# First group's stacks loaded in a place of their own, the last two gelu blocks moved beside attention, the last tile stored in halves

## The chip, the cores and the metric

The kernel runs on one core of a Trainium2 chip. Its engines are TensorE (PE in the profile, with PEld for its weight loads), VectorE (DVE), ScalarE (ACT), GpSimd (POOL) and SyncE (SP), which here only issues DMAs. The metric is the device time of one execution in microseconds (us), as the median of several runs.

## The reference

`x` has 2048 rows (tokens) and 512 columns, all float32. Two branches are computed from it and mixed row by row:

```python
g = sigmoid((x * gate_w).sum(-1, keepdims=True))
a = attention(x)      # 32 heads of 16 columns, softmax(q k^T / 4) v, then @ wo
h = layernorm(x)
u = gelu(einsum("bsd,sf->bdf", h, w1) + b1)   # over the tokens: S = 2048 -> F = 1792
b = einsum("bdf,fs->bds", u, w2) + b2         # F -> S
out = g * a + (1 - g) * b
```

## The kernel before

Every float32 matrix product is made from three products of rounded parts: a value is split into `hi` (a rounded copy, `float32r`) and `lo` (what is left), and `hi*hi`, `hi*lo` and `lo*hi` are summed in PSUM. `split` (L66 and L67) makes the two parts: the copy to `hi` is a CAST in the profile, the subtraction a TENSOR_TENSOR.

The work goes through these stages, one after another on TensorE:

1. **Transposes and v** (0 to about 52 us).
2. **Projections** of keys and of the first half of the queries (`project`, L358), until 122 us. Their parts go to DRAM (`kp`, `qp`). Layernorm of the first eight row chunks is made beside it (`ln_load`, `ln_rows`): rows `x` are loaded into three buffers, normalised into `hf`, and split into `h_hi` and `h_lo`.
3. **First layer of the mixer** (L449 to L469), until 277 us. The 1792 columns of w1 are done in blocks of 512, the last of 256: `n` = 4 (in the last block 2) accumulators `ps[i]` of one PSUM bank each, for 16 chunks of 128 rows, so there are 64 chunks in all, the last 16 of them half as wide. A chunk is `3 n` matmuls of 512 columns. Chunk by chunk a weight block is loaded (`w_raw`, four buffers, L145, SP queue), cast to `w_hi` on ACT and subtracted to `w_lo` on POOL (three buffers each); `weight()` works a few chunks ahead. When a block is done, its four accumulators go through `gelu` (L421), a generator of seven steps that is woven into the next blocks: the bias add on DVE (L426), a square on ACT (L428), two operations on DVE (L430, L431), tanh on ACT (L433), one operation on DVE (L435), the cast to `u_hi` on ACT (L437) and the subtraction to `u_lo` on DVE (L439). The gelu of the last two accumulators (blocks 12 and 13 of u) comes after the last chunk (L470).
4. **Attention and the second layer together** (L899 to L1047), until about 1245 us. There are 32 groups (two heads and half of the queries each) of four phases, so 128 phases; an order written out by hand (`manual_schedule`) fixes what each engine does when. A phase has 16 score matmuls, numbered n = 0 to 15 here (L982), each from the stacked keys `ks` and queries `qs` of its group into one of seven PSUM banks. DVE copies scores 1, 3, 5 and 7 to SBUF (`pe`, L999) and ACT takes their exponentials in one go at the end of the phase (L1014, 2048 columns). ACT takes scores 0, 2, 4, 6, 8 and 9 from PSUM one by one (L1003) and the rest in pairs (L944; in the first phase of a group one pair is taken as two singles, L947). Then 64 small matmuls (L872; 40 in the very first phase) multiply the exponentials by v into `av`, and DVE adds `av` to the group's sum (L894). Beside each score runs, on the other half of TensorE's rows, one matmul of the second layer or of another dense job, into the bank `dn` (L991). `calls` and `later` hold what is done at the start and at the end of a given phase; `second_layer(0)` is spread over phases 0 to 5 and reads blocks 12 and 13 of u in phases 4 and 5, and the first `late_query` (phases 6 and 7) reads `big0` and `big1`, which `load_xt` brings at phase 1 (L784).
5. **The end** (from `ps_end` to the last `finish`): the last groups are projected with wo, and `finish` (L1106) multiplies by the gate, adds the mixer's row tile and stores 128 rows of the output.

**The stacks around the change.** A group's stack `ks` is six DMAs of 128 KB and two memsets of 16 rows (`shift_rows`, L487); `qs` is eight DMAs of 64 KB (`stack`, L498). Before, `ks0`, `ks1` and two `qs` buffers lie in a pool `stk` (L480) that is opened after the first layer, at addresses that the first layer's `h_hi` and `h_lo` hold until their last chunks. The memsets of `ks0` are on POOL (L493), after the last weight split of the layer. The DMAs are issued at the start of the attention loop (L900), all on SP's one queue, in the order in which they are called.

Of the kernel before, what the change touches and what calls it, by code (L numbers as in the profile page):

```python
# [59 lines left out]
def gated_mix(ctx: ExitStack, tc: tile.TileContext, a_x, a_wqkv, a_wo, b_w1, b_b1, b_w2, b_b2, gate_w, out):  # L60
# [294 lines left out]
    bd.tile([P, 56], F32, name="pad", bufs=1)  # L355
    with tc.tile_pool(name="ln0", bufs=3, side="right") as ln:

# [18 lines left out]
        for b in range(ND):  # L376
            wk_b, wq_b = qk_w.pop(0), qk_w.pop(0)
            kmax = bd.tile([P, NQ], F32, name="kmax")
            for at, (n, keys) in enumerate(jobs):
# [12 lines left out]
                if at in (2, 5):  # L392
                    c = 2 * b + at // 3
                    ln_load(ln, c)
                    ln_rows(ln, c)
                if at in (3, 4):
# [16 lines left out]
    def layer(ps, hi, lo, rhs, first, last):  # L413
        for i, p in enumerate(ps):
            wh, wl = hi[:, i * P : (i + 1) * P], lo[:, i * P : (i + 1) * P]
            for k, (a, b) in enumerate(((wh, rhs[0]), (wh, rhs[1]), (wl, rhs[0]))):
                nc.tensor.matmul(p, a, b, start=first and k == 0, stop=last and k == 2)  # L417

    with tc.tile_pool(name="ln1", bufs=3, side="right") as ln, tc.tile_pool(name="gl", bufs=2, side="right") as gl:

# [22 lines left out]
        for c in range(AHEAD):  # L443
            ln_load(ln, NH + c, AHEAD + 1)


        STEPS = 7
        gelus = []
        for f0, cs in order.items():  # L449
            n = min(NB, F - f0) // P  # L450
            ps = [bank() for _ in range(n)]
            in_order = f0 == 0 or f0 + NB >= F
            if not in_order:
                for step in gelus:
                    list(step)
                gelus = []
            with tc.manual_schedule(engines=beside) if in_order else ExitStack():
                for at, c in enumerate(cs):
                    hi, lo = weight()

                    if f0 == 0 and AHEAD < c <= NH:
                        ln_load(ln, NH + c - 1, AHEAD + 1)
                    if f0 == 0 and AHEAD < c <= NH + AHEAD:
                        ln_rows(ln, NH + c - AHEAD - 1)
# [17 lines left out]
    out_pool = att_ctx.enter_context(tc.tile_pool(name="ot", bufs=2, reuse_waits="tile"))  # L482
    QW = 2 * NB
    NP = H // 2
    k_bufs = [stk.tile([P, S], F32R, name=f"ks{i}", bufs=1) for i in range(2)]

    def shift_rows(engine, t):  # L487
        for i in range(2):
            engine.memset(t[i * HALF + SHIFT[0] : i * HALF + SHIFT[0] + DH].bitcast(F32), -1.0)


    with tc.issue_after(subs[-1].ins):
        shift_rows(nc.gpsimd, k_bufs[0])  # L493


    landed = []

    def stack(dst, src, which, pair, planes):  # L498
        b, r0 = divmod(pair * 2 * DH, P)
        for i in range(2):  # L500
            rows = slice(r0 + i * DH, r0 + (i + 1) * DH)
            for row, *part in planes:
                at = slice(i * HALF + row, i * HALF + row + DH)
                landed.append(nc.sync.dma_start(dst[at].bitcast(F32), src[b][part[which], rows, :]))

    def load_k(g):
        t = k_bufs[g % 2]
        stack(t, kp_d, 1, g % NP, PAIRS)
        return t

    def load_q(g):
        half, pair = divmod(g, NP)
        t = stk.tile([P, QW], F32R, name="qs")
        stack(t, qp_d[half], 0, pair, [*PAIRS, SHIFT])
        return t
# [267 lines left out]

    call(1, load_xt, 2)  # L784
    for b in range(ND):
# [265 lines left out]
    with (  # L1051
# [161 lines left out]
```

## Time and profile before

| | |
|---|---|
| time, median of 3 runs | 1280.51 us (1280.42 to 1280.55) |
| the profiled execution | 1280.37 us, its span 1278.4 us |
| PE busy | 1262.8 us (99% of the span) |
| ACT busy | 1081.4 us (85%) |
| DVE busy | 684.0 us (54%) |
| POOL busy | 201.8 us (16%) |
| DMA | 152.35 MB, mean 119 GB/s |

The profile is that of one execution, and its times count from the start of its span. A row of a timeline has the start, the duration, the engine, the line, the operation, `out<-in` by the program's names with partitions and columns, the number of instructions merged into it, and in brackets how long the engine was idle before and what ended that wait. A row of the chain has start, duration and what ran; the chain is followed back from the last instruction, at each step to what released it. SPq and ACTq rows are DMA issues, not transfers.

### The profile page before, as it was taken

Reading aid. Unit: us, or ns where it says so; the run is one execution under the profiler, and the core shown is the slowest. Engines: PE = TensorE matmul, PEld = TensorE weight load, DVE = VectorE, ACT = ScalarE, POOL = GpSimd, SP = SyncE. Lnnn points to the kernel's source line nnn. Section 1 sums busy time; section 2 is a strip of 40 time slices with the busy share of each in tenths; the row PEclk is TensorE's granted clock in tenths of the full one; section 3 lists DMA queues with packets and bytes.
Section 4 is the critical chain, followed back from the end, with each engine's and each line's share of the span. In section 5 each row is a group of like instructions: output and inputs, shape, how many; then the busy total and the mean of one; then the engine's idle time right before and its main releaser. Section 6 shows DMA issues by size and latency. Waiting matters only on the chain.

```text
span 1278.4 us, 33281 instructions
## 1 busy us (share of the span) xinstructions
PE 1262.8 (99%) x13342; PEld 835.1 (65%) x13342; DVE 684.0 (54%) x1149; ACT 1081.4 (85%) x1569; POOL 201.8 (16%) x318
## 2 busy tenths in 40 slices
PE   9999999989999999999999999999999999999998
PEld 7888888865666666666666666666666666666556
DVE  5675444174546454545555465545554455457663
ACT  4443344269999999999999999999999999999990
POOL 0220444462010111010101101111111111000000
PEclk9999999989999999999999999999999999999999
DMA  4798533255654454554343444443553443366611
GB/s 132 263 332 294 165 92 90 83 128 154 182 132 99 88 105 82 155 93 96 76 97 91 94 102 83 88 87 70 115 101 67 86 110 64 55 160 182 147 58 69
DMA packets 100559, 152.35 MB, mean 119 GB/s; under 512 B 17109, under 2 KB 56171, under 8 KB 96300
## 3 DMA queue, kind: packets, MB, share of 16 engines
q1 hardware_dynamic: 99820, 149.08, 46.5%
q8 instruction: 108, 1.77, 0.6%
q10 hardware_dynamic: 576, 1.05, 0.2%
q14 instruction: 55, 0.45, 0.1%
HBM read 105.39 MB, written 44.68 MB: 117 GB/s over the span
## 4 chain that ended last, share of the span: by engine, by line
PE 97%; ACT 1%; DMA 1%; issue 0%; DVE 0%; SPq 0%; ACTq 0%
PE av L872 30%; PE s L982 24%; PE acc L417 12%; PE t L982 12%; PE acc L74 8%; PE s L872 5%; PE dn L991 3%; PE pa L1065 2%; ACT p L944 1%; PE acc L198 1%; PE acc L267 0%; DMA qs<-qp 0%; ACT p L1003 0%; DMA ks<-kp 0%; ACT pe L1014 0%
## 5 line engine op out<-in xcount | busy, mean ns | idle before, releaser
L1003 ACT ACTIVATE p<-s 128x512 f32<-128x512 f32 x768 | 416.5, 809 | 1.6 <-PE s L982 1.6
L944 ACT ACTIVATE p<-t 128x1024 f32<-128x1024 f32 x352 | 369.3, 1290 | 0.0
L982 PE MATMUL s<-qs,ks 64*128 64x512 f32 x1344 | 345.5, 401 | 6.7 <-DMA qs<-qp 6.1
L999 DVE COPY pe<-s 128x512 f32<-128x512 f32 x512 | 318.4, 684 | 8.4 <-PE s L982 7.8
L982 PEld LDWEIGHTS s<-qs,ks 64*128 64x128 f32 x1344 | 239.3, 185 | 101.5 <-issue 51.9
L872 PE MATMUL av<-p,v 128*32 128x256 f32 x4904 | 288.1, 379 | 0.0
L1014 ACT ACTIVATE pe<-pe 128x2048 f32<-128x2048 f32 x129 | 279.8, 2172 | 0.0
L894 DVE TENSOR_TENSOR ot<-av,ot 128x512 f32<-128x512 f32 (+2 forms) x140 | 84.8, 606 | 364.1 <-PE av L872 363.8
L872 PEld LDWEIGHTS av<-p,v 128*32 128x32 f32 x4904 | 159.4, 110 | 105.3 <-ACT p L1003 0.3
L991 PE MATMUL dn<-u_hi,w_hi 64*128 64x512 f32 x448 | 183.4, 409 | 0.0
L991 PE MATMUL dn<-u_lo,w_hi 64*128 64x512 f32 x448 | 182.6, 408 | 0.0
L991 PE MATMUL dn<-u_hi,w_lo 64*128 64x512 f32 x448 | 181.8, 406 | 0.0
L982 PE MATMUL t<-qs,ks 64*128 64x512 f32 x704 | 179.3, 442 | 1.7
L67 POOL TENSOR_TENSOR w_lo<-w_raw,w_hi 128x512 fp32r<-128x512 f32 (+1 forms) x128 | 152.9, 1200 | 121.9 <-ACT w_hi L66 100.6
L982 PEld LDWEIGHTS t<-qs,ks 64*128 64x128 f32 x704 | 89.9, 184 | 86.6 <-ACT p L1003 86.6
L995 POOL MEMSET token<- 1x1 f32 x128 | 11.4, 89 | 834.8 <-PE dn L991 786.1
L872 PE MATMUL av<-pe,v 128*32 128x256 f32 x2048 | 137.3, 385 | 0.1
L66 ACT CAST w_hi<-w_raw 128x512 fp32r<-128x512 f32 (+1 forms) x67 | 38.0, 569 | 81.9 <-PE acc L417 62.6
L872 PEld LDWEIGHTS av<-pe,v 128*32 128x32 f32 x2048 | 53.5, 109 | 54.8 <-ACT p L1003 32.3
L417 PE MATMUL acc<-h_hi,w_hi 128*128 128x512 f32 x224 | 87.9, 392 | 0.0
L417 PE MATMUL acc<-h_hi,w_lo 128*128 128x512 f32 x224 | 87.8, 392 | 0.0
L417 PE MATMUL acc<-h_lo,w_hi 128*128 128x512 f32 x224 | 87.8, 392 | 0.0
(152 smaller groups left out, 1479.7 us busy)
## 6 DMA issues: line engine op xcount, KB each, us to landing
w_raw<-in_B_w_dram SPq DMA_DIRECT2D x96, 256.0 KB
ks<-kp SPq DMA_DIRECT2D x192, 128.0 KB
qs<-qp SPq DMA_DIRECT2D x256, 64.0 KB
x<-in_A_x_dram SPq DMA_DIRECT2D x32, 256.0 KB
kp<-pc SPq DMA_DIRECT2D x16, 512.0 KB
qp<-pc SPq DMA_DIRECT2D x8, 768.0 KB
qp<-row SPq DMA_DIRECT2D x24, 256.0 KB
v<-v SPq DMA_DIRECT2D x4, 1088.0 KB
```

What stands on the lines that cost most here:

```text
L66: copy(hi, src)
L67: return sub(lo, src, hi.bitcast(F32), ALU.subtract)
L74: nc.tensor.matmul(ps, a, b, start=start and n == 0, stop=stop and n == last)
L417: nc.tensor.matmul(p, a, b, start=first and k == 0, stop=last and k == 2)
L872: mm = nc.tensor.matmul(av[32 * j : 32 * (j + 1), i * QC : (i + 1) * QC], vb[b][:, v_at : v_at + 32], pt[:, h * QC : (h + 1) * QC], start= ...
L894: nc.vector.tensor_tensor(x, y, x, ALU.add)
L944: nc.scalar.activation(pt, twos[low, low + 1], AF.Exp, scale=SCALE)
L982: nc.tensor.matmul(s, kt[grp][rows_i, c * P : (c + 1) * P], qt[grp][rows_i, qb * NB : (qb + 1) * NB], start=True, stop=True,)
L991: mm = nc.tensor.matmul(ps, a[half], b[half], start=begin and not second, stop=last and bool(second))
L999: nc.vector.tensor_copy(pt, s)
L1003: nc.scalar.activation(pt, s, AF.Exp, scale=SCALE)
L1014: nc.scalar.activation(x, x, AF.Exp, scale=SCALE)
```

## The change

- `first_stacks`, a pool that is open from stage 2 on, holds `ks` (8 KB a partition) and `qs` (4 KB). Until the layernorm is done the same place holds its rows: four buffers `x` in `ks` (`ln_load`) and two `hf` in `qs` (`ln_rows`), in place of the pools `ln0` and `ln1`.
- At the start of the second block of the first layer (`f0 == NB`), `first_loads` sets the shift rows of `ks` on DVE and issues the 14 loads of group 0's stacks on SP. Group 1's `ks1` and `qs1` stay in `stk`; the two `qs` buffers alternate by hand.
- In the last block of the layer, `layer` goes through its two accumulators in reverse, so `ps[1]` is finished three matmuls before `ps[0]`.
- The gelu of blocks 12 and 13 is taken apart: the two bias adds stay at the end of the layer, on DVE, `ps[1]` first (`late_u`); `inner` (three DVE operations; the square is now one of them) is put at the end of phase 0 for both blocks, `tanh` (ACT) at the end of phase 1 for both, `outer` (three DVE operations; the cast to `u_hi` is now on DVE) at the end of phase 2 for the one and of phase 3 for the other. Their intermediate result is `late_s`, in the place of `big0`.
- `load_xt(2)`, which fills `big0` and `big1`, is called at phase 3 instead of phase 1.
- The bank `dn` is taken from the other end of PSUM.
- The last output tile is multiplied and stored in two halves of 256 columns, the first from ACT's queue, the second from SP's.

```diff
+    first_stacks = ctx.enter_context(tc.tile_pool(name="fs", bufs=1, reuse_waits="tile"))
+    ln_x = first_stacks.tile([P, S], F32, name="ks").rearrange("p (n d) -> p n d", d=D)
+    ln_h = first_stacks.tile([P, QW], F32, name="qs").rearrange("p (n d) -> p n d", d=D)
-    def ln_load(ln, c, bufs=3):
-        xs[c] = ln.tile([P, D], F32, name="x", bufs=bufs)
+    def ln_load(c):
+        xs[c] = ln_x[:, c % 4, :]
         nc.sync.dma_start(xs[c], xf[c * P : (c + 1) * P, :])
-    def ln_rows(ln, c):
-        hf = ln.tile([P, D], F32, name="hf", bufs=2)
+    def ln_rows(c):
+        hf = ln_h[:, c % 2, :]
...
     def layer(ps, hi, lo, rhs, first, last):
-        for i, p in enumerate(ps):
+        for i, p in list(enumerate(ps))[:: 1 if len(ps) == NB // P else -1]:
...
+        def first_loads():
+            k_bufs.append(first_stacks.tile([P, S], F32R, name="ks"))
+            q_bufs.append(first_stacks.tile([P, QW], F32R, name="qs"))
+            shift_rows(nc.vector, k_bufs[0])
+            return {0: load_k(0)}, {0: load_q(0)}
...
+            if f0 == NB:
+                kt, qt = first_loads()
...
-        for step in gelus:
-            list(step)
...
-    with tc.issue_after(subs[-1].ins):
-        shift_rows(nc.gpsimd, k_bufs[0])
...
+    late_u = []
+    for i, p in reversed(list(enumerate(ps))):
+        u = out_pool.tile([P, D], F32, name="row", bufs=3)
+        at = NF - len(ps) + i
+        nc.vector.tensor_scalar_add(u, p, b1[:, at : at + 1])
+        late_u.append((u, at))
+    late_s = o_pool.tile([P, ND, NB], F32, name="big0")
+    def inner(i):
+        u, s = late_u[i][0], late_s[:, i, :]
+        nc.vector.tensor_mul(s, u, u)
+        nc.vector.tensor_scalar(s, s, GELU_A, 1.0, ALU.mult, ALU.add)
+        nc.vector.tensor_mul(s, s, u)
+    def tanh(i):
+        nc.scalar.activation(late_s[:, i, :], late_s[:, i, :], AF.Tanh, scale=GELU_C)
+    def outer(i):
+        u, at = late_u[i]
+        nc.vector.scalar_tensor_tensor(u, late_s[:, i, :], 1.0, u, ALU.add, ALU.mult)
+        split(u_hi[:, at, :], u_lo[:, at, :], u, nc.vector.tensor_copy, nc.vector.tensor_tensor)
...
-    ps_dn = psum_ctx.enter_context(tc.tile_pool(name="ps_dn", bufs=1, space=PSUM, reuse_waits="tile"))
+    ps_dn = psum_ctx.enter_context(tc.tile_pool(name="ps_dn", bufs=1, space=PSUM, side="right", reuse_waits="tile"))
...
-    call(1, load_xt, 2)
+    for i in range(2):
+        on_dve(0, inner, i)
+        on_dve(1, tanh, i)
+        on_dve(2 + i, outer, i)
+    call(3, load_xt, 2)
...
-        kt, qt = {0: load_k(0)}, {0: load_q(0)}
...
-        for t, queue in ((1, nc.sync), (3, nc.scalar), (5, nc.sync), (7, nc.scalar)):
+        for t, queue in ((1, nc.sync), (3, nc.scalar), (5, nc.sync)):
             finish(t, queue)
+        row, gate, dst = row_of(7)
+        for cols, queue in ((slice(0, D // 2), nc.scalar), (slice(D // 2, D), nc.sync)):
+            nc.vector.scalar_tensor_tensor(row[:, cols], pa[7][:, cols], gate, row[:, cols], ALU.mult, ALU.add)
+            queue.dma_start(dst[:, cols], row[:, cols])
```

More of the change, by code (lines that the diff above doesn't have):

```diff
@@ L355, in gated_mix @@
     bd.tile([P, 56], F32, name="pad", bufs=1)
-    with tc.tile_pool(name="ln0", bufs=3, side="right") as ln:
+    if True:
         def project(w, n):
@@ L393, in gated_mix @@
                     c = 2 * b + at // 3
-                    ln_load(ln, c)
-                    ln_rows(ln, c)
+                    ln_load(c)
+                    ln_rows(c)
                 if at in (3, 4):
@@ L417, in layer @@
                 nc.tensor.matmul(p, a, b, start=first and k == 0, stop=last and k == 2)
-    with tc.tile_pool(name="ln1", bufs=3, side="right") as ln, tc.tile_pool(name="gl", bufs=2, side="right") as gl:
+    with tc.tile_pool(name="gl", bufs=2, side="right") as gl:
         def gelu(ps, fb):
@@ L443, in gated_mix, with shift_rows, stack, load_k @@
         for c in range(AHEAD):
-            ln_load(ln, NH + c, AHEAD + 1)
+            ln_load(NH + c)
+        def shift_rows(engine, t):
+            for i in range(2):
+                engine.memset(t[i * HALF + SHIFT[0] : i * HALF + SHIFT[0] + DH].bitcast(F32), -1.0)
+        landed = []
+        def stack(dst, src, which, pair, planes):
+            b, r0 = divmod(pair * 2 * DH, P)
+            for i in range(2):
+                rows = slice(r0 + i * DH, r0 + (i + 1) * DH)
+                for row, *part in planes:
+                    at = slice(i * HALF + row, i * HALF + row + DH)
+                    landed.append(nc.sync.dma_start(dst[at].bitcast(F32), src[b][part[which], rows, :]))
+        def load_k(g):
+            t = k_bufs[g % 2]
+            stack(t, kp_d, 1, g % NP, PAIRS)
+            return t
+        def load_q(g):
+            half, pair = divmod(g, NP)
+            t = q_bufs[g % 2]
+            stack(t, qp_d[half], 0, pair, [*PAIRS, SHIFT])
+            return t
+        k_bufs, q_bufs = [], []
+        def first_loads():
[3 more added lines that the diff above has]
+            return {0: load_k(0)}, {0: load_q(0)}
         STEPS = 7
@@ L461, in gated_mix @@
                     if f0 == 0 and AHEAD < c <= NH:
-                        ln_load(ln, NH + c - 1, AHEAD + 1)
+                        ln_load(NH + c - 1)
                     if f0 == 0 and AHEAD < c <= NH + AHEAD:
-                        ln_rows(ln, NH + c - AHEAD - 1)
+                        ln_rows(NH + c - AHEAD - 1)
                     layer(ps, hi, lo, (h_hi[c], h_lo[c]), at == 0, at == NS - 1)
@@ L482, in gated_mix @@
     out_pool = att_ctx.enter_context(tc.tile_pool(name="ot", bufs=2, reuse_waits="tile"))
[L483 to L489, printed above, removed]
-    with tc.issue_after(subs[-1].ins):
-        shift_rows(nc.gpsimd, k_bufs[0])
[L496 to L515, printed above, removed]
+    k_bufs.append(stk.tile([P, S], F32R, name="ks1", bufs=1))
+    q_bufs.append(stk.tile([P, QW], F32R, name="qs1", bufs=1))
     def second_out(t, ps):
@@ L782, in put_whole @@
         return put(steps, at, [len(steps)])
-    call(1, load_xt, 2)
+    for i in range(2):
+        on_dve(0, inner, i)
+        on_dve(1, tanh, i)
+        on_dve(2 + i, outer, i)
+    call(3, load_xt, 2)
     for b in range(ND):
```

2 lines of the change are left out of this document (added).

## The prediction

> **What bounds the kernel now.** I read the page's chain first, by engine, then the same chain in order of time where its PE pieces are broken.
>
> ```profile
> span 1278.4 us, 33281 instructions
> ...
> PE 97%; ACT 1%; DMA 1%; issue 0%; DVE 0%; SPq 0%; ACTq 0%
> ```
>
> ```profile
> 274.70 3.76 DMA ks<-kp
> ...
> 278.48 4.82 DMA qs<-qp
> 283.30 0.76 PE s L982
> ...
> 291.46 0.50 PE s L982
> ...
> 299.86 0.43 PE s L982
> ...
> 307.35 0.42 PE s L982
> ...
> 314.83 0.43 PE s L982
> ```
>
> TensorE carries 97% of the chain, and the DMA's 1% lies almost wholly in one place: 8.6 us (274.70 to 283.30) in which the stacks of group 0 arrive. The five PE rows start phases 0 to 4. Phases 2 and 3 take 7.49 and 7.48 us; phase 0 takes 8.16 and phase 1 8.40. So the transition costs an idle time and two slow phases. The waits of 270 to 300 us name what ended last, and the windows give the granted clock (the third figure from the end):
>
> ```profile
> PEld s L982 <- POOL ks L489: 6.5, 1, 6.5
> PE s L982 <- DMA qs<-qp: 6.1, 1, 6.1
> ```
>
> ```profile
> 280.50:283.30 2.80, 0.00 (x1) 0.04 (x1) 2.67 (x5) 1.57 (x3) 2.69 (x3) 0.50 0.98 152
> 283.30:287.20 3.90, 3.90 (x18) 3.90 (x20) 3.10 (x6) 2.60 (x5) 1.09 (x1) 0.50 0.55 116
> ```
>
> The queries' DMA came last and the POOL memset of the shift rows shortly before. Through the idle time the clock fell to 0.50, and the first 3.9 us of phase 0 ran at half speed. What follows is set by ACT:
>
> ```profile
> 275.70 0.62 ACT L66 CAST w_hi<-w_raw 128x512 fp32r<-128x512 f32 x1 [0.22 <-PE acc L417]
> ...
> 287.51 1.09 ACT L1003 ACTIVATE p<-s 128x512 f32<-128x512 f32 x2 [0.26 <-PE s L982]
> ...
> 293.04 3.10 ACT L1003 ACTIVATE p<-s 128x512 f32<-128x512 f32 x6
> 295.90 2.99 ACT L944 ACTIVATE p<-t 128x1024 f32<-128x1024 f32 x3
> ...
> 300.41 3.21 ACT L1003 ACTIVATE p<-s 128x512 f32<-128x512 f32 x6
> ```
>
> ACT waits for PE up to score 8 (287.51), then has no gap. It starts the exponentials of phase 1 at 293.04, 1.58 us after PE began that phase; for phase 2 the distance is 0.55 us (300.41 against 299.86). A distance larger by 1.03 us made phase 1 longer by 0.91 us: where ACT is late, PE pays nearly all of it. That is the price for any work put on ACT here.
>
> **The change part by part.** *The first score.* The last matmul of the first layer:
>
> ```profile
> 276.81 0.39 PE L417 MATMUL acc<-h_hi,w_lo 128*128 128x512 f32 x1
> ```
>
> With stacks and shift rows landed 100 us earlier, score 0 follows at the layer's spacing of 0.23 us, at 277.04. In the changed program it waits only for these DMAs, for the shift rows' memsets and for a DVE evacuation of the block before. What is late next is score 1: it reuses the bank of `ps[1]` and waits for its bias add; behind it stands all of phase 0 on PE. DVE's order there, then, with rows for the later steps:
>
> ```profile
> 275.51 1.37 DVE L439 TENSOR_TENSOR u_lo<-gu,u_hi 128x512 fp32r<-128x512 f32 x1 [0.71 <-ACT u_hi L437]
> 276.80 1.40 DVE L426 TENSOR_SCALAR gu<-acc,b 128x512 f32<-128x512 f32 x2
> 278.24 0.43 DVE L430 TENSOR_SCALAR gs<-gs 128x512 f32<-128x512 f32 x1
> 278.70 0.69 DVE L431 TENSOR_TENSOR gs<-gs,gu 128x512 f32<-128x512 f32 x1
> 279.31 1.49 DVE L430 TENSOR_SCALAR gs<-gs 128x512 f32<-128x512 f32 x1
> ...
> 300.62 2.48 DVE L999 COPY pe<-s 128x512 f32<-128x512 f32 x4
> ```
>
> The two bias adds are the pair at 276.80, 0.70 us each, in the new order: `ps[1]` is out at 277.5, `ps[0]` at 278.2. Score 1 comes at 277.55 instead of 277.27; the reversed order in `layer` keeps this at 0.3 us. Score 6, which needs the other bank, comes at 278.7 anyway.
>
> *ACT in phase 0.* Its third cast for the second layer has to wait for the last chunk and starts at about 277.1; at 0.5 us before the next can begin, it leaves ACT free as score 0 is ready, 277.6. Four gelu steps that stood here (two squares, two tanh) and two casts are gone. Score 2 is ready about 278.3 (issued 277.8, 0.39 us of matmul, 0.1 to be seen); from there ACT runs without a gap at 0.48 us each (295.90 less 293.04, over six), so score 8's exponential is at 278.3 + 3 x 0.48 = 279.75 instead of 287.51. The rest of the phase is unchanged: 293.04 - 287.51 = 5.53. Phase 1 starts on ACT at 285.3 instead of 293.04: 7.75 us gained, of which 6.26 is idle time, the rest slow clock and the gelu work that stood in between.
>
> *Tanh in phase 1.* 300.41 - 293.04 = 7.37 us as before, plus two tanh of 512 columns. The step of two ACT operations from SBUF to SBUF is bounded by the exponentials' 0.48 and by the whole duration of such a cast; a pair gives the value:
>
> ```profile
> 170.34 1.14 ACT L437 CAST u_hi<-gu 128x512 fp32r<-128x512 f32 x2
> ```
>
> 1.14 - 0.62 = 0.52 each, 1.04 for both (bounds 0.95 and 1.25). Nothing hides it, as ACT has no gap. Phase 2's exponentials begin at 285.3 + 7.37 + 1.04 = 293.7 instead of 300.41: **6.7 us gained**, and the later phases keep their pace.
>
> *DVE in phases 0 to 3.* Four copies 2.48, two `inner` of 0.46 + 0.61 + 0.61 = 1.7 (starts 278.24, 278.70, 279.31; the square priced as the multiplication), one add of half a bank, taken at 0.43 like the shortest of these rows: from 278.2 to 284.5. PE starts phase 1 at 291.46 - 7.75 = 283.7, its score 1 is ready at 284.5, so the next copy is not late. `outer` is three operations, by the rows above between 0.43 and 1.49 each, in a phase of 7.49 us in which the copies take 2.48: hidden, and due only in phase 4.
>
> *Queues.* SP: `load_xt` waits for the last `outer` in phase 3, about 305 on the new clock; behind it on SP stand group 2's queries and the projection weights, which are not needed before phases 6 to 8.
>
> ```profile
> 290.45 0.84 SPq L543 DMA_DIRECT2D big<-xt  x2
> ...
> 294.00:301.00 7.00, 7.00 (x90) 4.02 (x90) 2.17 (x5) 7.00 (x11) 0.82 (x2) 1.00 0.90 328
> 302.00:306.00 4.00, 4.00 (x58) 2.28 (x58) 1.10 (x2) 4.00 (x8) 0.09 (x1) 1.00 0.01 2
> ```
>
> Issued at 290.45, the 2 MB were in by 302, 12 us; 305 + 12 = 317, and phase 6 begins about 323: 6 us of cover. The first layer's loads move too: the rows `x` go ahead of weight blocks (into windows where PE has no idle time to lose), and group 0's 14 DMAs (1.28 MB) go ahead of weight chunk 20:
>
> ```profile
> 157.35 11.72 SPq L145 DMA_DIRECT2D w_raw<-in_B_w_dram  x5
> 172.02 0.62 ACT L66 CAST w_hi<-w_raw 128x512 fp32r<-128x512 f32 x1 [0.54 <-POOL w_lo L67]
> ```
>
> ```profile
> 160.00:168.00 8.00, 8.00 (x36) 6.45 (x35) 3.31 (x6) 3.75 (x6) 3.37 (x4) 1.00 0.33 98
> ```
>
> One load each 2.8 us; chunk 20 is the third of these five, issued at 163, cast at 172.02 and used at about 177.6 (two chunks of 2.8 us on). If the burst takes the 8.6 us that it took at 274.70 and most of it is issued by 160.3, chunk 20 is issued at 169 and in by 172: cost nothing.
>
> *The last tile.*
>
> ```profile
> 1271.08 0.33 SPq L1109 DMA_DIRECT2D out_dram<-base  x1
> ...
> 1273.08 0.75 DVE L1108 SCALAR_TENSOR_TENSOR base<-pa,g,base 128x512 f32<-128x512 f32 x1 [2.03 <-PE pa L1065]
> 1273.86 0.34 ACTq L1109 DMA_DIRECT2D out_dram<-base  x1
> ```
>
> ```profile
> 1271.70:1272.80 1.10, 1.10 (x6) 0.76 (x4) 0.00 (x0) 0.00 (x0) 0.00 (x0) 1.00 0.62 238
> 1274.20:1276.20 2.00, 0.00 (x0) 0.00 (x0) 0.00 (x0) 0.00 (x0) 0.00 (x0) 1.00 0.43 152
> ```
>
> The last 256 KB were on the move for 2.0 us, the tile before for 1.1. Half a tile saves between nothing and 1.0; I take half of the shorter, 0.55, less 0.05 for two shorter DVE operations instead of one: **0.5 us**. [...]
>
> **Sum:** 6.7 + 0.5 = 7.2 us. Against the profiled execution, 1280.37 (span 1278.4 and 1.97 around it, taken as unchanged), that is 1273.2; this execution lies 0.14 below the median of the runs shown, which the range covers.
>
> **Rivals.** *1. DVE gets late beside POOL* (gain 4.8, 1275.6). POOL's memsets for `ks1` (3.6 us) move with phase 0's end and now lie beside `inner`:
>
> ```profile
> 278.79 1.73 POOL L67 TENSOR_TENSOR w_lo<-w_raw,w_hi 128x512 fp32r<-128x512 f32 x1 [0.78 <-ACT w_hi L66]
> 280.57 3.82 POOL L489 MEMSET ks<- 16x2048 f32 x2
> ```
>
> ```profile
> 281.44 1.47 DVE L435 SCALAR_TENSOR_TENSOR gu<-gs,gu 128x512 f32<-128x512 f32 x2
> ```
>
> The same DVE operation that took 0.43 took 1.49 (279.31) beside the POOL subtraction at 278.79. Two `inner` scalings each held by a whole memset (1.9) make DVE late by up to 3.8; 1.4 of that is slack (PE's score 8 of phase 1, held by ACT until 286.3, needs the copy of score 1, due 284.9), the rest, 2.4, is paid. Against it: the two DVE operations at 281.44, beside that very memset, kept 0.7 us each, though they are not this operation. The Trainium skill's page "SBUF — State Buffer", section "Who interferes with whom", speaks for it: a scaling from SBUF to SBUF may use the port pair shared with GpSimd, and who comes second waits for the whole instruction. No run here yet has the pair side by side.
>
> *2. The gain is larger* (up to 8.3, 1272.1): the store saves 1.0 and tanh hides in a gap of ACT.
>
> *3. It does not do what it says* (within 2.5 us, about 1279): another input of phase 0 is late, for instance the second layer's weights, and PE waits at 277 after all. Against it: their second cast stands at 275.70 in the trace, before the layer's end.
>
> *4. Slower* (1284 or more): weight chunk 20, stuck behind the 14 stack loads on SP. It costs only from the point at which the load lands later than 175.5 (cast and subtraction before 177.6), and the sign turns when PE loses over 7.2 us, so when the burst takes some 20 us instead of 8.6. DMA was busy a third of the time there (0.33 in the window above), which speaks against it; the burst's 16-row DMAs, which run slower than the weights', speak for it.
>
> **How the numbers follow.** Forecast (gain 6.2 to 7.9) 0.62; rival 1 and dearer tanh together 0.22; rival 2 0.08; rival 3 0.04; rival 4 0.04. The range runs from rival 2 (with 0.4 us more) to rival 1 (with 0.7 more): 1271.7 to 1276.3. Faster by over 0.2% (2.56 us, about what a measurement of this kernel can tell from no change): all but rivals 3 and 4, 0.92; within 0.2% 0.04; slower 0.04.
>
> **What would show it.** Right: first score near 277.1 and the granted clock at 1.0 throughout; second score about 0.5 after it, released by a DVE add; phases 1 and 2 both near 8.4 us, with tanh between the last exponential of phase 1 and the first of phase 2; phase 3 starts near 300.6 instead of 307.35 and phases of 7.49 from there. Wrong: a wait of PE inside 122 to 277 us, a score of phase 1 released by a DVE copy, a table load between the exponentials, a wait for `big` in phase 6, or last packets as long as before.

## The result, and the profile after

The changed kernel takes **1282.38 us** (median of 20 executions, 1280.67 to 1283.80), the kernel before 1280.36 us (median of 20, 1279.49 to 1281.33): a ratio of 1.0015, 95% interval 1.0008 to 1.0021. The change makes the kernel 2.0 us slower; 1273.2 was forecast. The profiled execution of the changed kernel took 1280.95 us (span 1279.1) and is among the shortest of its 20; what the others have besides is found below.

Its page, the span and the chain by engine:

```profile
span 1279.1 us, 33309 instructions
...
PE 96%; issue 1%; ACT 1%; DVE 1%; POOL 0%; POOLq 0%; DVEq 0%
```

The DMA's 1% is gone from the chain, as the change intended: nothing waits for the first stacks any more. But "issue" (time for which the profile finds nothing that was waited for), DVE and POOL have come in. Three places hold the loss. The first is inside the first layer; the chain in order of time (start, duration, what):

```profile
172.34 6.99 issue
...
179.38 1.28 POOL w_lo L67
```

the timeline of POOL, which says what POOL stood waiting for in these 6.99 us:

```profile
179.37 3.77 POOL L67 TENSOR_TENSOR w_lo<-w_raw,w_hi 128x512 fp32r<-128x512 f32 x3 [7.43 <-ACT w_hi L66]
```

and the timeline of PE there and at the layer's end:

```profile
177.35 0.39 PE L423 MATMUL acc<-h_hi,w_lo 128*128 128x512 f32 x1
179.34 0.50 PE L423 MATMUL acc<-h_hi,w_hi 128*128 128x512 f32 x1 [1.61 <-ACT w_hi L66]
...
180.70 0.50 PE L423 MATMUL acc<-h_hi,w_lo 128*128 128x512 f32 x1 [0.62 <-POOL w_lo L67]
...
279.75 0.39 PE L423 MATMUL acc<-h_hi,w_lo 128*128 128x512 f32 x1
280.07 0.50 PE L1015 MATMUL s<-qs,ks 64*128 64x512 f32 x1
```

PE stands idle for 1.61 and 0.62 us, first for a cast of weights on ACT and then for a subtraction on POOL; the layer ends at 280.14 instead of 277.20. From the first to the last of its 672 matmuls it takes 157.65 us instead of 154.84, 2.8 more. Score 0 then follows at once. Its successors, in the chain of 277 to 305 us:

```profile
284.19 1.95 DVE big L541
...
288.80 0.43 DVE ot L928
...
289.27 0.50 PE s L1015
...
295.84 0.43 PE s L1015
...
303.77 0.43 PE s L1015
```

Phase 2 starts at 295.84 (299.86 before), phase 3 at 303.77 (307.35 before). Counted from the layer's end, phase 3 comes after 23.63 us instead of 30.15: the 6.5 us that the moved stacks and the moved gelu were to bring are there.

The second place is the end of the loop. Timeline of the changed kernel, then of the kernel before:

```profile
1241.47 1.35 PE L906 MATMUL av<-pe,v 128*32 128x256 f32 x16
...
1242.88 0.76 DVE L928 TENSOR_TENSOR ot<-av,ot 128x256 f32<-128x256 f32 x2 [1.73 <-PE av L906]
...
1243.79 0.93 PE L1098 MATMUL pa<-big,e 128*128 128x512 f32 x3 [0.97 <-DVE ot L928]
```

```profile
1244.75 1.33 PE L872 MATMUL av<-pe,v 128*32 128x256 f32 x16
...
1246.02 0.96 PE L1065 MATMUL pa<-big,e 128*128 128x512 f32 x3
```

Before, `pa` followed `av` without a gap; now it waits 0.97 us for DVE. The third place is behind the last matmul. The last matmul of the kernel before:

```profile
1272.18 0.86 PE L1065 MATMUL pa<-big,e 96*128 96x512 f32 x3
```

Timeline of the changed kernel, PE, DVE and the queues' issues:

```profile
1268.82 0.33 SPq L1142 DMA_DIRECT2D out_dram<-base  x1
...
1269.92 0.86 PE L1098 MATMUL pa<-big,e 96*128 96x512 f32 x3
1270.82 0.87 DVE L1162 SCALAR_TENSOR_TENSOR base<-pa,g,base 128x256 f32<-128x256 f32 x2 [2.03 <-PE pa L1098]
1271.33 0.34 ACTq L1163 DMA_DIRECT2D out_dram<-base  x1
1271.72 0.33 SPq L1163 DMA_DIRECT2D out_dram<-base  x1
```

The windows behind it (the last two columns are the DMA engines' busy share and GB/s):

```profile
1272.00:1273.70 1.70, 0.00 (x0) 0.00 (x0) 0.00 (x0) 0.00 (x0) 0.00 (x0) 1.00 0.50 164
1273.70:1275.00 1.30, 0.00 (x0) 0.00 (x0) 0.00 (x0) 0.00 (x0) 0.00 (x0) 0.82 0.02 6
```

The last packets of the output have ended by 1273.7, 2.9 us after the last matmul (1270.78), where it was 3.2 before (1276.2 after 1273.04). Yet the span ends at 1279.1, 8.3 us after that matmul, where it was 5.4. So the two profiled executions differ, place by place:

| | before | after | difference |
|---|---|---|---|
| last matmul of the first layer ends | 277.20 | 280.14 | +2.94 |
| from there to phase 3 | 30.15 | 23.63 | -6.52 |
| phase 3 to the last `av` | 938.73 | 939.05 | +0.32 |
| last `av` to the first `pa` | -0.06 | 0.97 | +1.03 |
| first `pa` to the last matmul's end | 27.02 | 26.99 | -0.03 |
| last matmul to the end of the span | 5.41 | 8.31 | +2.90 |
| sum | | | +0.64 |

Of the first row 0.13 us lies ahead of the layer; its start varies between 122.36 and 123.14 us in the 13 profiles of this case. What is gained once is given back in three places, none of them in attention's phases.

### The profile page after: what moved, and what is told of

Its sections match the earlier page's. It is cut to its first block, busy times and chain, and to the rows that moved or that the text cites. A ratio compares the mean times of both kernels' runs of the same rounds, so it can differ in the third digit from the quotient of the medians.

```text
span 1279.1 us, 33309 instructions
## 1 busy us (share of the span) xinstructions
PE 1263.5 (99%) x13342; PEld 832.5 (65%) x13342; DVE 688.6 (54%) x1156; ACT 1079.2 (84%) x1565; POOL 197.8 (15%) x316
## 4 chain that ended last, share of the span: by engine, by line
PE 96%; issue 1%; ACT 1%; DVE 1%; POOL 0%; POOLq 0%; DVEq 0%
PE av L906 30%; PE s L1015 23%; PE t L1015 12%; PE acc L423 12%; PE acc L74 8%; PE s L906 5%; PE dn L1024 3%; PE pa L1098 2%; PE acc L198 1%; PE acc L267 0%; ACT p L977 0%; ACT pe L1047 0%; PE pa L1128 0%; ACT p L1036 0%; PE acc L244 0%
## 5 line engine op out<-in xcount | busy, mean ns | idle before, releaser
L977 ACT ACTIVATE p<-t 128x1024 f32<-128x1024 f32 x352 | 367.0, 1271 | 0.0
```

Of the source, the lines that this page charges most:

```text
L977: nc.scalar.activation(pt, twos[low, low + 1], AF.Exp, scale=SCALE)
```

## The experiments

Each run is compared with executions of the kernel before on the same chip, whose medians were 1280.36 to 1280.44. "Tail" is the time from the end of the last matmul to the end of the span in the profiled execution.

| run | time, us | range | ratio to before, interval | tail |
|---|---|---|---|---|
| changed kernel | 1282.38 | 1280.67 to 1283.80 | 1.0015 (1.0008 to 1.0021) | 8.31 |
| a_whole | 1279.92 | 1277.97 to 1281.20 | 0.9989 (0.9980 to 0.9998) | 6.05 |
| b_act2 | 1279.25 | 1278.10 to 1281.14 | 0.9990 (0.9981 to 0.9999) | 6.66 |
| c_inorder | 1278.44 | 1277.96 to 1278.70 | 0.9983 (0.9974 to 0.9992) | 8.50 |
| d_bank | 1280.38 | 1279.81 to 1282.63 | 1.0002 (0.9993 to 1.0011) | 8.18 |
| e_all | 1274.31 | 1274.27 to 1274.78 | 0.9952 (0.9938 to 0.9965) | 5.72 |
| f_inner | 1275.12 | 1274.62 to 1275.28 | 0.9956 (0.9942 to 0.9970) | 5.81 |
| g_gelu | 1279.77 | 1278.21 to 1280.14 | 0.9991 (0.9982 to 1.0000) | 5.62 |
| h_spread | 1274.86 | 1274.50 to 1275.12 | 0.9955 (0.9942 to 0.9969) | 5.95 |
| j_sp | 1276.95 | 1276.67 to 1277.73 | 0.9974 (0.9964 to 0.9984) | 8.10 |
| k_act5 | 1274.54 | 1274.35 to 1274.78 | 0.9955 (0.9939 to 0.9972) | 5.87 |
| m_memset | 1274.48 | 1273.91 to 1275.15 | 0.9954 (0.9938 to 0.9971) | 5.57 |

**The stall in the first layer (c_inorder).** ACT's timeline in the changed kernel shows why the cast came late:

```profile
169.96 0.61 ACT L66 CAST w_hi<-w_raw 128x512 fp32r<-128x512 f32 x1
170.47 1.14 ACT L443 CAST u_hi<-gu 128x512 fp32r<-128x512 f32 x2
173.85 1.29 ACT L434 ACTIVATE gs<-gu 128x512 f32<-128x512 f32 x2 [2.23 <-DVE gu L432]
175.70 0.64 ACT L439 ACTIVATE gs<-gs 128x512 f32<-128x512 f32 x1 [0.56 <-DVE gs L437]
176.76 0.63 ACT L439 ACTIVATE gs<-gs 128x512 f32<-128x512 f32 x1 [0.43 <-DVE gs L437]
177.37 0.62 ACT L443 CAST u_hi<-gu 128x512 fp32r<-128x512 f32 x1
178.15 0.62 ACT L443 CAST u_hi<-gu 128x512 fp32r<-128x512 f32 x1 [0.17 <-DVE gu L441]
178.68 1.65 ACT L66 CAST w_hi<-w_raw 128x512 fp32r<-128x512 f32 x3
```

Before, casts stood at 172.02 and 176.11, between these gelu steps; the second of them in ACT's timeline of the kernel before:

```profile
176.11 0.60 ACT L66 CAST w_hi<-w_raw 128x512 fp32r<-128x512 f32 x1
```

Now the three casts come behind all of them, one after another and without a wait of their own: their data had been there (the last packets of the burst and of the three weight loads behind it ended at 172.4). In this block the order on ACT is not written out but made by the scheduler when the kernel is built, and with the burst ahead of the weights it put two casts behind six gelu operations. Why it chose this order is not shown; that the order is the cause is tested here and in h_spread below. The experiment keeps the burst and writes the order out:

```diff
-            in_order = f0 == 0 or f0 + NB >= F
+            in_order = f0 <= NB or f0 + NB >= F
```

> The changed kernel with the second block of the first layer in a written order on ACT, DVE and POOL too (one step of each gelu a chunk, as in the first and the last block); the 14 stack loads stay together where they are. In the changed kernel PE stood idle for 2.2 us at 178 to 181, and the cast of weight chunk 20 started at 178.68, though the packets of its load ended at 172.4. Theory (the order in which ACT takes its work): the cast comes right after the load, the idle time goes, the layer ends at 277.2 instead of about 280 and the time falls by 2.5 us (2.0 to 2.9). Rival (the load is late, or the weight pipeline has run dry behind the burst): an idle time of PE of 1 us or more remains between 172 and 190, released by a cast that itself waits for a DMA; the time falls by less than 1.2 us.

Measured: 1278.44 us, 3.9 below the changed kernel, where 2.0 to 2.9 were expected. The burst is in the same place (its issues at 156.14 to 167.50, in the changed kernel at 155.69 to 167.88), PE has no gap, and the layer ends at 277.78, 154.84 us after its start, as long as before the change. ACT's timeline:

```profile
172.59 0.62 ACT L66 CAST w_hi<-w_raw 128x512 fp32r<-128x512 f32 x1 [2.10 <-PE acc L423]
...
175.31 0.62 ACT L66 CAST w_hi<-w_raw 128x512 fp32r<-128x512 f32 x1 [1.57 <-POOL w_lo L67]
...
178.03 0.62 ACT L66 CAST w_hi<-w_raw 128x512 fp32r<-128x512 f32 x1 [1.57 <-POOL w_lo L67]
```

One cast each 2.7 us, waiting for PE or POOL and never for a DMA: the burst delays nothing, the order does. The theory holds. The gain is 1.1 us more than the 2.8 of the stall, and the range shrank from 3.1 to 0.7 us; the next runs show why.

**What the stall costs besides (a_whole, b_act2, d_bank).** These three keep the stall, and each of their profiled executions has a stretch of half clock behind it, which the profiled execution of the changed kernel has not. Windows of a_whole (the third figure from the end is the granted clock):

```profile
178.00:182.00 4.00, 1.77 (x7) 1.10 (x7) 1.76 (x3) 2.52 (x5) 2.28 (x2) 1.00 0.02 2
182.00:185.40 3.40, 3.40 (x10) 2.67 (x9) 0.00 (x0) 0.62 (x1) 1.65 (x3) 0.51 0.71 192
```

and the same stretch of the changed kernel:

```profile
182.00:185.40 3.40, 3.40 (x17) 2.81 (x16) 0.00 (x0) 0.62 (x1) 2.43 (x2) 1.00 0.69 208
```

10 matmuls instead of 17 in 3.4 us. The layer takes 159.25 us in a_whole and 159.06 and 159.07 in b_act2 and d_bank, against 157.65 in the changed kernel's profile. So the stall costs 2.8 us always and 1.4 to 1.6 more in the executions that the clock catches. That most of the 20 executions of the changed kernel belong to these is not shown by a profile of theirs, but their times fit: 13 took 1282.22 us or more and 7, the profiled one among them, 1281.83 or less. So do the ranges: 2.8 to 3.2 us in the four kernels with the stall, 0.4 to 1.2 in those without (g_gelu aside, which has a half clock elsewhere).

What decides whether the clock catches a stall can be read from the traces. In all 13 the granted clock changes only at whole multiples of 3.413 us from its first change (in a_whole at 4.58, 182.07 and 185.48 us). Divide PE's timeline into stretches of that length, from one possible change to the next, and add up PE's idle time in each: among the stretches at full clock, every one with 1.66 us or more was followed by half clock, and none with 1.63 us or less. In the changed kernel the stall fell into two stretches, with 1.13 and 1.10 us of idle time; in a_whole one stretch held 1.66, in b_act2 and d_bank 1.86. The first change lies between 4.04 and 7.09 us in the 13 profiles, so the same stall can fall either way. This is an inference from one execution of each kernel, with idle times taken from matmul ends that the profile models.

The Trainium skill's page "TensorE: Matmul & The Clock Gate", section "Part 1: The HAM clock gate (the "warmup" mystery)", has the clock halved after at least one idle window of about 3.4 us, in windows that run freely. The stretches of 3.413 us and the half clock in some profiles only agree; but here a window with 1.66 us of idle time, with matmuls beside it, was enough.

**The tail.** Three runs tell the queue from the halving. First the last tile whole on ACT's queue, as before:

```diff
-        for t, queue in ((1, nc.sync), (3, nc.scalar), (5, nc.sync)):
+        for t, queue in ((1, nc.sync), (3, nc.scalar), (5, nc.sync), (7, nc.scalar)):
             finish(t, queue)
-        row, gate, dst = row_of(7)
-        for cols, queue in ((slice(0, D // 2), nc.scalar), (slice(D // 2, D), nc.sync)):
...
```

> The changed kernel with its last tile multiplied and stored whole on ACT's queue again; nothing else differs. In the profile of the changed kernel 8.27 us pass from the first multiplication of the last tile (1270.82) to the end of the span (1279.09), before it were 5.36 (1273.08 to 1278.44), though the last packets of the tile land earlier. Theory: SP, which now issues the last store, comes later to the branch behind the last store and has to fetch the code behind it; then the distance falls back to 5.4 (5.1 to 5.7) and the time by 2.9 us against the changed kernel (1278 in the profiled run). Rival 1, the two narrow transfers are dear: the same here, told apart by the next run. Rival 2, the long end comes with the earlier end of PE or with the place of the code: the distance stays over 7.5 and the time within 0.5 us.

Measured: the tail is 6.05 us, 2.3 less (2.9 were expected; with a whole tile on ACT last the tails lie between 5.41, the kernel before, and 6.05), the time 1279.92, 2.5 below the changed kernel (both with the stall and its clock). Then both halves, but both from ACT:

```diff
-        ... ((slice(0, D // 2), nc.scalar), (slice(D // 2, D), nc.sync)):
+        ... ((slice(0, D // 2), nc.scalar), (slice(D // 2, D), nc.scalar)):
```

> The changed kernel with both halves of the last tile stored from ACT's queue, none from SP's. Theory (SP's late branch): SP is through its wait list early, ACT's branch comes at about 1.85 us after the first multiplication and its code 2.75 us later as in the kernel before, so the distance is 5.3 to 5.8 and the time 2.5 to 3.0 us below the changed kernel. Rival 1 (narrow rows of 1 KB are dear, whichever queue issues them): the distance stays at 7.8 to 8.3 and the time within 0.5 us of the changed kernel.

Measured: a tail of 6.66 us, between what the two theories gave, but 1.6 below halves on two queues; 1279.25 us. Why not 5.3 to 5.8 shows in ACT's issues:

```profile
1272.89 2.05 ACTq L1163 DMA_DIRECT2D out_dram<-base  x2
```

Two issues that take 0.34 us each alone span 2.05: the second took 1.62. By the trace's semaphore and branch records SP then waits last for ACT, which stands still behind its branch from 1275.53 to 1278.08. Halving is not free, then, but small. The clean test is a whole tile on SP, in the kernel with all three repairs (e_all, below):

```diff
-        for t, queue in ((1, nc.sync), (3, nc.scalar), (5, nc.sync), (7, nc.scalar)):
+        for t, queue in ((1, nc.scalar), (3, nc.sync), (5, nc.scalar), (7, nc.sync)):
```

> The run with all three repairs, but with the queues of the last four tiles exchanged: 1 and 5 on ACT's, 3 and the whole last tile 7 on SP's. No tile is halved. From the last matmul to the end of the span it was 5.7 us with all repairs and 8.2 to 8.5 in the runs whose second half went out on SP. Theory (SP as issuer of the last store comes late to the code behind the branch, where it alone has a list of sixteen waits): 8.0 to 8.9 us, the time 2.3 to 3.2 us above the run with the repairs (1274.3). Rival (halving was what cost): 5.5 to 6.0 us and the same time within 0.4.

Measured: a tail of 8.10 us, and 1276.95, 2.6 above e_all. SP's last issue and the last matmul in j_sp, then in e_all:

```profile
1265.94 0.86 PE L1099 MATMUL pa<-big,e 96*128 96x512 f32 x3
...
1267.61 0.33 SPq L1143 DMA_DIRECT2D out_dram<-base  x1
```

```profile
1264.88 0.33 SPq L1143 DMA_DIRECT2D out_dram<-base  x1
...
1265.98 0.86 PE L1099 MATMUL pa<-big,e 96*128 96x512 f32 x3
```

From SP's last issue to the end of the span it is 7.3 us in j_sp (1274.9), 7.4 in the changed kernel (1271.72 to 1279.1), 7.2 in d_bank and 7.6 in c_inorder, with halves and without. The trace's semaphore and branch records say what fills it. Behind its last store SP branches past a general version of attention that isn't run here (1272.66 in the changed kernel), stands still until 1275.41, goes through six waits of 0.1 us, stands still again from 1275.83 to 1277.59, and does ten more. All that it still has to wait for had landed before the first pause ended (the last store at 1274.1), and both pauses have instruction packets in them. In e_all the first pause, 2.7 us from 1265.89, lies beside the last matmul and the issue of the last store; the next stop, 1.7 us from 1268.84, is the wait for that store, which lands at 1270.5; and behind the eighth wait, where j_sp stands still for 1.6 us, it is 0.4. Before the change SP's last store was tile 5's, 2.0 us ahead of the end of the last matmul, so that its pauses lay beside other work; it waited for the last store until 1276.74 and last of all for ACT, which stood still behind its own branch from 1274.79 to 1277.54. SP's waits ended at 1277.6, 4.5 us after the last matmul. The halved tile put SP's last issue 0.9 us behind the last matmul, and its own pauses now end last: its waits are over at 1278.2, 7.4 us after the last matmul. That is the 2.9 us.

Whether SP can be freed still earlier, with tile 5 on ACT as well:

```diff
-        ... ((1, nc.sync), (3, nc.scalar), (5, nc.sync), (7, nc.scalar)):
+        ... ((1, nc.sync), (3, nc.scalar), (5, nc.scalar), (7, nc.scalar)):
```

> The run with all three repairs, but with tile 5 on ACT's queue too, so that SP's last store is tile 1's, 5.6 us earlier. Theory: SP has all its code long before the last store lands, so its pauses at 1268.84 and 1270.81 shrink to the wait for the store itself and the end comes 5.1 to 5.7 us after the last matmul: the same time to 0.6 us less than with the repairs. Rival (two stores one behind the other on ACT: the second issue took 1.62 us instead of 0.34 when both halves went that way): the last store leaves ACT 1.3 us later and the time is 0.7 to 1.3 us longer.

Measured: 1274.54 and a tail of 5.87, the same as e_all within its range. SP starts on its waits early (1262.66), but waits for the last store all the same, until 1270.61. The second issue on ACT took no longer this time, 2.8 us behind the first; so the 1.62 us of b_act2 goes with two issues close together (0.44 us from start to start). What held the second one there is not shown.

The Trainium skill's page "Perfetto Trace Analysis", section "DMA Optimizations", says that splitting a DMA may let the whole complete sooner where the DMA engines are mostly idle. They are nearly idle here (busy share 0.07 from 1271 to 1272 us in the changed kernel), and the last packets did end sooner, 2.9 us after the last matmul instead of 3.2. But neither split made the program end sooner: tails of 8.2 to 8.5 us on two queues and 6.7 on one, against 5.4 to 6.05 unsplit on ACT.

**The bank (d_bank).** The part of the change that the prediction gave no price:

```diff
-        pa = [ps_end.tile([P, D], F32, name=f"pa{t}") for t in range(8)]
+        pa = [ps_end.tile([P, D], F32, name=f"pa{t}") for t in (1, 2, 3, 4, 5, 6, 7, 0)]
+        pa = pa[-1:] + pa[:-1]
```

> The changed kernel with the end's accumulator pa0 put into the bank of dn (which is free) and the other seven moved up by one, as the banks stood before the change; nothing else differs. In the changed kernel the first pa matmul waited 0.97 us for DVE's ot, which reads the last av out of the same bank. Theory: the wait is gone, the first pa matmul follows av within 0.1 us and the time falls by 1.0 us (0.8 to 1.2). Rival: the chain from ot over the sums and the reciprocals sets the end whatever pa0 does, so the idle time only moves to a later matmul and the time falls by less than 0.4.

Measured, in the timeline of PE in d_bank:

```profile
1243.08 1.33 PE L906 MATMUL av<-pe,v 128*32 128x256 f32 x16
...
1244.33 0.96 PE L1099 MATMUL pa<-big,e 128*128 128x512 f32 x3
```

The wait is gone, and from the end of `av` to the end of the last matmul it is 26.95 us instead of 27.96: 1.0 us, as expected, with nothing behind it that took its place. The medians differ by 2.0, but both kernels still have the stall and the half clock that comes in some executions only.

**All three repairs (e_all).** Its edit is that of c_inorder, a_whole and d_bank together.

> The changed kernel with all three repairs: block 2 of the first layer in a written order, the last tile whole on ACT's queue, pa0 in the bank of dn. If the three losses are separate (theory), the gains add up: from 1278.4 (written order alone) less 2.3 (the end of 8.5 us becomes one of 6.05, as in the run with the whole tile) less 1.0 (bank) = 1275.1, within 0.6, and with it the 5 us of gain that the prediction sought are there. Rival: the losses cover each other (an earlier end of PE only waits longer for the code or the store); then it stays above 1276.5.

Measured: 1274.31 us, 0.9952 of the time before (0.9938 to 0.9965), with five executions within 0.5 us. That is 8.1 us below the changed kernel and 0.8 below the 1275.1 that was expected, 0.2 outside the margin; half a microsecond of it is the tail, which fell by 2.8 us from c_inorder's 8.50 and not by 2.3. The three losses are separate and add up. This version beats both kernels; it is 6.1 us below the kernel before, where the prediction sought 7.2.

**The burst itself (h_spread).** Instead of the written order, the 14 loads one by one:

```diff
-                    landed.append(nc.sync.dma_start(dst[at].bitcast(F32), src[b][part[which], rows, :]))
+                    put_off(nc.sync.dma_start, dst[at].bitcast(F32), src[b][part[which], rows, :])
...
+                    if f0 >= NB and todo and at % 2 == 0:
+                        start, operands = todo.pop(0)
+                        landed.append(start(*operands))
                     layer(ps, hi, lo, (h_hi[c], h_lo[c]), at == 0, at == NS - 1)
```

> Not the written order, but the other two repairs, and the 14 stack loads one by one, in every second chunk of the first layer's blocks 2 and 3 instead of all at once; the scheduler then puts the casts of weight chunks 20 and 21 on ACT where they were before the change. Theory (the place of the casts is the cause, which the scheduler chose from its own estimate of the burst): no idle time of PE at 178, the same time as with the written order within 0.4 us. Rival (the burst as such disturbs the weights): with the loads spread it is over 0.5 us faster than the written order, or, if a single stack load in front of a weight load is enough, an idle time remains.

Measured: 1274.86, no gap of PE in the layer, 0.55 above e_all (up to 0.4 was expected). The profiled executions differ by 0.12 ahead of the layer, by 0.23 in the tail and by 0.18 in the loop; no wait in the trace accounts for it, and it is left at that. Either way of keeping the casts in place ends the stall.

**DVE in phase 0 (f_inner, m_memset).** Rival 1 of the prediction did appear: `inner`'s first scaling took 1.94 us, and PE stood idle for 0.90 us in phase 1 behind a late DVE. First, less for DVE in phase 0:

```diff
-        on_dve(0, inner, i)
-        on_dve(1, tanh, i)
+        on_dve(i, inner, i)
+        on_dve(1 + i, tanh, i)
```

> The run with all three repairs, but with inner and tanh of the second of the two late blocks one phase later (phases 1 and 2 instead of 0 and 1), so that DVE has 2.0 us less to do in phase 0, where it held the ot addition back until 288.80 and PE stood idle for 0.90 us in phase 1. Theory (ACT is the bound there, it had no gap from 288.28 to 296): the idle time of PE shrinks and the time is the same within 0.3 us. Rival (rival 1 of the prediction, a late DVE is paid by PE): 0.6 to 0.9 us faster than the run with the three repairs.

Measured: the gap of PE shrinks from 0.90 to 0.40; from the layer's end to phase 4 it is 30.88 us against 31.04 in e_all: 0.16 less, so the idle time was worth next to nothing. The median, 1275.12, is 0.8 above e_all; by the profiled executions 0.6 of that arises ahead of the layer and 0.4 behind phase 4, which the edit doesn't touch. Then POOL's memset out of the way:

```diff
-            if p == 0:
+            if p == 2:
                 shift_rows(nc.gpsimd, k_bufs[1])
```

> The run with all three repairs, but with POOL's two memsets of ks1's shift rows after phase 2 instead of after phase 0. The first inner's scaling on DVE took 1.94 us in phase 0, beside a memset of 1.9 us; the second took 0.68. Theory (DVE's scaling is held while the memset runs): the first now takes 0.43 to 0.7, the ot addition comes about 1.3 to 1.5 us earlier and the idle time of PE in phase 1 (0.90) goes; the time stays within 0.3 us, as ACT is what bounds phase 1. Rival (the scaling is slow by itself, or by the copies before it): it still takes over 1.5 us.

Measured: 1274.48, the same as e_all. PE's idle time in phase 1 did not go but shrank to 0.40 us, in which PE waits for ACT, and phase 4 comes 30.88 us after the layer's end, as in f_inner. DVE and POOL in the changed kernel:

```profile
284.19 1.94 DVE L541 TENSOR_SCALAR big<-big 128x512 f32<-128x512 f32 x1
```

```profile
284.04 3.83 POOL L455 MEMSET ks<- 16x2048 f32 x2
```

and DVE in m_memset:

```profile
281.95 0.43 DVE L541 TENSOR_SCALAR big<-big 128x512 f32<-128x512 f32 x1
...
283.75 0.43 DVE L541 TENSOR_SCALAR big<-big 128x512 f32<-128x512 f32 x1
```

The scaling is held while the first memset runs (it ends at 285.84, the scaling at 286.13) and takes 0.43 without it. That settles the mechanism of rival 1, and its price: no more than 0.2 us, since ACT bounds phase 1 and has no gap there. The rule that the prediction cited from the Trainium skill's page "SBUF — State Buffer" agrees: who comes second waits for the whole instruction.

**The moved gelu (g_gelu).** e_all with the gelu of the last two blocks at the end of the layer again; only the stacks are early:

```diff
+        for step in reversed(gelus):
+            list(step)
     h_ctx.close()
...
-    late_u = []
...
-        on_dve(0, inner, i)
-        on_dve(1, tanh, i)
-        on_dve(2 + i, outer, i)
-    call(3, load_xt, 2)
+    call(1, load_xt, 2)
```

> The run with all three repairs, but with the gelu of the last two blocks whole at the end of the layer on ACT and DVE as before the change (load_xt at phase 1 again); only the stacks are early. It tells what the moved gelu is worth. Theory (a chain): ACT takes its exponentials behind the last of these casts, and one block takes about 4.4 us from its bias add to its cast, both overlapped 5.5 us, so phase 1 starts about 4.9 us later, less the 1.0 of two tanh in phase 1: 3.9 us slower (3.0 to 5.0). Rival (only the work of ACT counts): six operations of 0.52 us come, two tanh of 0.52 go: 2.1 us slower. Second rival (the early stacks are worth nothing without the moved gelu): 6 us slower or more.

Measured: 1279.77, 5.5 above e_all, half a microsecond more than the chain's upper bound. From the layer's end to phase 3 it is 28.67 us, against 23.56 in e_all and 30.1 before. ACT's steps stand between the exponentials, which lets PE idle for 1.38, 1.06 and 1.16 us, and the clock halves once more:

```profile
280.00:284.40 4.40, 1.76 (x10) 0.67 (x8) 4.40 (x8) 3.69 (x8) 0.00 (x0) 1.00 1.07 219
284.40:291.30 6.90, 5.94 (x46) 2.86 (x46) 2.01 (x4) 5.68 (x7) 3.69 (x3) 0.51 0.98 298
```

So early stacks alone are worth 1.4 us and the moved gelu 5.1 more: the idle time before score 0 merely moved behind it.

## Why the prediction was wrong, step by step

- **The first score.** Right. Score 0 starts 0.32 us after the start of the last layer matmul (0.23 forecast), and score 1 waits 0.3 us for the bias add. That this is at 280.07 and not at 277.04 is the layer's lateness.
- **ACT in phase 0 and tanh in phase 1.** Right. Set 2.94 us later for the layer, phase 1's exponentials were due at 288.24 and came at 288.28; phase 2's were due at 296.6 and came at 296.99, in which the two tanh took the 1.04 that was forecast (295.95 to 296.99). The rest of phase 1 on ACT took 7.67 us and not 7.37:

```profile
288.28 3.27 ACT L1036 ACTIVATE p<-s 128x512 f32<-128x512 f32 x6
...
295.95 1.18 ACT L545 ACTIVATE big<-big 128x512 f32<-128x512 f32 x2
296.99 3.06 ACT L1036 ACTIVATE p<-s 128x512 f32<-128x512 f32 x6
```

- **DVE in phases 0 to 3, rival 1.** The mechanism was rival 1's, not the forecast's: DVE came late, held by the memset, and a DVE addition released a score of phase 1. But the price of 2.4 us was wrong; at most 0.2 was paid, as ACT was the bound. On PE phase 1 took 9.0 us and phase 2 7.9, where both were to take 8.4. The forecast of 6.7 us for the transition met 6.5.
- **Queues: "chunk 20 is issued at 169 and in by 172: cost nothing".** Failed, and not in its arithmetic: SP issued it at 168 and its packets had ended by 172.4. It took the cast's and the use's place from the profile of before, as if the order on ACT stayed. The new order put two casts behind six gelu operations: 2.8 us, and 1.4 to 1.6 more of half clock in three of the four profiled kernels with this order. Rival 4 named the place and the wrong mechanism (a load that lands late).
- **A step that isn't there: the bank.** The prediction took `dn`'s move to the other end of PSUM as nothing and never asked which tile then shares a bank with which: 1.0 us at the end of the loop.
- **"The last tile": saves 0.5.** Wrong in sign: it costs 2.9 (2.6 in the clean test). The transfer did become shorter and ended earlier after the last matmul. What the step left out is what the issuing queue has to do afterwards. The profile of before had the clue: packets until 1276.2, an end at 1278.4, and SP's last issue at 1271.08.
- **The sum.** -6.5 for the transition (6.7 forecast); +2.8 stall, +1.0 bank, +2.9 tail (-0.5 forecast), and 0.4 of small shifts (0.1 ahead of the layer, 0.3 in the loop) make +0.6 in the profiled execution. The rest of the measured 2.0 is, by the times and not by a profile, the half clock. Without the three losses, e_all's 1274.31 lies 1.1 above the forecast.

## What to carry to other kernels

Where a scheduler makes the order, a moved DMA can move other engines' instructions: compare the order of every engine around the place before pricing it, above all where PE's weights are prepared. Price a store at the end by what its issuing engine must still do after it, not by its bytes. And when a pool changes sides, list which tiles now share a bank and who reads the old one last.

## What the runs showed of the hardware that was not expected

- The same stall of PE (1.61 and 0.62 us idle within 3.0) was followed by 3.41 us at a clock of 0.50 in the profiles of a_whole, b_act2 and d_bank and not in that of the changed kernel. In the 13 profiles the clock changes only in steps of 3.413 us, and a stretch of that length at full clock was followed by half clock with 1.66 us of idle time or more in it, and not with 1.63 or less.
- The end of the program is 7.2 to 7.6 us behind SP's last DMA issue where SP issues last, whatever it stores; 4.3 to 4.7 of it are two pauses with instruction packets in them. From the last matmul it is then 8.1 to 8.5 us, and 5.4 to 6.05 where ACT issues a whole tile last.
- Two DMA issues in a row on ACT's queue took 0.34 and 1.62 us; 2.8 us or more apart, 0.34 each.
- A DVE scaling of 128x512 from SBUF to SBUF took 0.43 us alone and 1.94 beside a POOL memset of 16x2048.
